# Batch 3's loads gated on the second half of batch 2's q^T in an attention kernel with a feed-forward stage

## The chip, the cores and the metric

One core of a Trainium2 chip. The metric is device time in microseconds (us) of one execution. Times are medians over several executions of the same kernel, with the lowest and highest where that matters.

## The reference

```python
# q, k, v: (batch 8, heads 8, seq 1024, head_dim 64); E, F: (64, 1024)
k_proj = einsum('ks,bhsd->bhkd', E, k)          # 1024 keys become 64
v_proj = einsum('ks,bhsd->bhkd', F, v)
attn   = softmax(q @ k_proj^T / 8)
x      = (attn @ v_proj).transpose(0, 2, 1, 3).reshape(8192, 512)
out    = maximum(x @ w1, x @ w2) @ w_out        # (8192, 512), float32
```

## The kernel before

TensorE carries the whole kernel: projections, scores, values and the feed-forward products of one batch are interleaved by hand in a fixed order of "slots". The attention of batch b runs among the feed-forward products of the batch before it. What the argument needs is who moves the data of the next batch.

**GpSimd issues the loads**, 1 MB each, in the order k, v, q. Four buffers rotate among all k, v and q tiles, so a load must wait until the last reader of the buffer that it takes over is done.

```python
kvq = ctx.enter_context(tc.tile_pool(name="kvq", bufs=4))
...
def step_gate(t, n, *at):        # a 1x1 copy: GpSimd stands here until that part of the tile is written
    nc.gpsimd.tensor_copy(out=junk, in_=t[n][(slice(0, 1), *at, slice(0, 1))])
```

**SyncE issues the transposes by DMA and all stores**, in one queue, in order. q^T comes in two halves (heads 0 to 3 and heads 4 to 7); from batch 3 on the projected keys are transposed by DMA too (kpt).

```python
def step_qt_dma(t, h0=0, h1=H):
    nc.sync.dma_start_transpose(out=t["qt"][:, h0:h1]..., in_=t["q"][:, h0:h1]...)   # cut
def step_kpt_dma(t):
    nc.sync.dma_start_transpose(out=t["kpt"], in_=t["kp"]...)                        # cut
```

**The schedule.** `("P", 0, p, i)` is a slot of the down products of the first unit (half a batch), `("U", n, h, i)` one of the up products under unit n, `("G", n, h)` the place of a group of scores. The line marked "the gate: head 3" is the one that the change touches. (Comments are added, and the lines that set up a batch's tiles are cut.)

```python
t = tiles[2]
at_slot(("P", 0, 1, 0), step_qt_dma, t, 0, H // 2)              # first half of q^T
at_slot(("U", 1, 0, 1), step_kv, t, 0, H, "kv", True)
at_slot(("U", 1, 0, 4), step_kpt, t, 0, H, True)                # batch 2: kpt by TensorE
at_slot(("G", 1, 0), step_qt_dma, t, H // 2, H)                 # second half, behind the stores
at_slot(("U", 1, 0, 6), step_gate, t, "qt", H // 2 - 1)         # the gate: head 3
at_slot(("U", 1, 0, 6), loads, 3, "k", "v", "q")

for b in range(3, B):
    t = tiles[b]; n = 2 * b - 3
    key = ("G", n, 0) if b == 3 else ("U", n - 1, 1, 5)
    at_slot(key, step_qt_dma, t, 0, H // 2)
    at_slot(key, step_qt_dma, t, H // 2, H)
    at_slot(("U", n, 0, 1), step_kv, t, 0, H, "kv", True, True) # its end issues kpt by DMA
    at_slot(("U", n, 0, 6), step_gate, t, "qt", H - 1)          # the gate: head 7
    at_slot(("U", n, 0, 6), step_gate, t, "kp", H - 1, 1)
    at_slot(("U", n, 0, 6), loads, b + 1, "k", "v", "q")
```

From batch 3 on, both halves of q^T, then a store, then kpt go through SyncE's queue, and the first scores of the batch need kpt.

The softmax here doesn't subtract the row's maximum and nothing guards it: scores larger than these inputs give would overflow.

Of the kernel before, what the change touches and what calls it, by code (L numbers as in the profile page):

```python
# [16 lines left out]
def kernel(  # L17
# [14 lines left out]
    B, H, S, D = q.shape  # L32
# [436 lines left out]
    U = {(b, o): {"n": n, "b": b, "o": o, "t": tiles[b]} for n, (b, o) in enumerate(units)}  # L469
# [263 lines left out]
    t = tiles[0]  # L733
# [100 lines left out]
    def at_slot(key, s, *a):  # L834
        steps.setdefault(key, []).append(lambda: s(*a))
# [11 lines left out]
    t = tiles[1]  # L847
# [26 lines left out]
    t = tiles[2]  # L874
# [2 lines left out]
    at_slot(("U", 1, 0, 1), step_kv, t, 0, H, "kv", True)  # L877
    at_slot(("U", 1, 0, 4), step_kpt, t, 0, H, True)
    at_slot(("G", 1, 0), step_qt_dma, t, H // 2, H)
    at_slot(("U", 1, 0, 6), step_gate, t, "qt", H // 2 - 1)  # L880
    at_slot(("U", 1, 0, 6), loads, 3, "k", "v", "q")

    for b in range(3, B):
        t = tiles[b]
# [77 lines left out]
```

## Time and profile before

| | before |
|---|---|
| median of 3 runs | 325.81 us (325.14 to 325.97) |
| span of the profiled run, its clock | 323.2 us, 1.000 |
| TensorE busy | 316.0 us, 98% |

The prediction shows most of the lines of this kernel's profile. Here are those that it left out. First, from the page, the granted TensorE clock in 40 slices (9 is 90% or more of full speed), and the chain that ended last by engine:

```profile
PEclk9999999999999999999999999999999999999999
...
PE 84%; DMA 9%; DVE 2%; POOL 2%; issue 1%; SPq 1%; ACT 0%; DVEq 0%; POOLq 0%
```

The clock is full throughout and the chain is TensorE's own work for 84% of the span. The waits of TensorE after 60 us (line, releaser, then us in total, times, longest):

```profile
PE mm_ps L275 <- DMA qt_sb<-q_sb: 0.3, 1, 0.3
```

In 260 us TensorE waits once, for 0.3 us. The DMA queues from 77.9 to 81.7 us (packets, MB, share of the 16 engines):

```profile
DMA packets 562, 0.56 MB, mean 148 GB/s; under 512 B 28, under 2 KB 561, under 8 KB 561
...
q0 software_dynamic: 465, 0.48, 91.8%
```

q0 is GpSimd's queue of loads.

### The profile page before, as it was taken

To read this page: it belongs to the slowest core of one execution; us is meant where nothing else is said; L and a number is where in the kernel's file an instruction comes from. 1 tells how busy PE (TensorE), PEld (TensorE's weight loads), DVE (VectorE), ACT (ScalarE), POOL (GpSimd) and SP (SyncE) were. 2 spreads that over 40 slices of the span, in tenths; PEclk is the share of its full clock that TensorE was granted. 3 is DMA by queue.
4 is the path that set the end of the run, shared out by engine and by line. 5 is a ranking of instruction groups with operands and counts; after the bars stand their busy time and mean duration, and the time that the engine had idled before them with its cause. 6 is when DMAs were issued, how large, how long until landed. Compare 5 with 4: busy or idle time off the path is not lost.

```text
span 323.2 us, 9033 instructions
## 1 busy us (share of the span) xinstructions
PE 316.0 (98%) x3852; PEld 248.4 (77%) x3852; DVE 236.8 (73%) x420; ACT 203.1 (63%) x364; POOL 41.6 (13%) x65
## 2 busy tenths in 40 slices
PE   8989999999999999999999999999999999999995
PEld 3554457878887888878887888878887888888884
DVE  1365798896867797877967796977967796969572
ACT  1466532667676777667776777657776777764541
POOL 8649002001200300030000300030000000000000
PEclk9999999999999999999999999999999999999999
DMA  8999999999999799699979999689969130312133
GB/s 160 207 196 185 204 204 204 207 203 179 256 216 213 135 203 244 143 177 144 234 147 201 154 211 231 115 180 183 232 130 213 38 100 32 99 34 98 34 121 108
DMA packets 76280, 53.14 MB, mean 164 GB/s; under 512 B 29520, under 2 KB 76112, under 8 KB 76240
## 3 DMA queue, kind: packets, MB, share of 16 engines
q0 software_dynamic: 30976, 28.31, 56.0%
q1 hardware_dynamic: 45264, 24.25, 31.2%
q8 instruction: 30, 0.49, 0.6%
q14 instruction: 10, 0.08, 0.1%
HBM read 57.15 MB, written 16.78 MB: 229 GB/s over the span
## 4 chain that ended last, share of the span: by engine, by line
PE 84%; DMA 9%; DVE 2%; POOL 2%; issue 1%; SPq 1%; ACT 0%; DVEq 0%; POOLq 0%
PE mm_ps L649 43%; PE mm_ps L571 24%; PE att_ps L188 4%; DMA v_sb<-in_v_dram 4%; DMA qt_sb<-q_sb 3%; PE mm_ps L415 3%; PE att_ps L287 3%; PE mm_ps L275 3%; PE mm_ps L453 2%; DMA big<-in_moe_w_dram 2%; POOL q_sb L102 1%; POOL k_sb L102 1%; DVE gt_sb L586 1%; PE mm_ps L246 1%; PE mm_ps L440 1%
## 5 line engine op out<-in xcount | busy, mean ns | idle before, releaser
L542 ACT COPY p_sb<-mm_ps 128x512 f32<-128x512 f32 x172 | 97.2, 594 | 42.0 <-PE mm_ps L571 30.0
L649 PEld LDWEIGHTS <-big 128*128 128x128 f16 x768 | 73.5, 98 | 12.0 <-issue 3.5
L649 PE MATMUL mm_ps<-T_sb,big 128*128 128x256 f16 x576 | 77.9, 273 | 0.0
L586 DVE TENSOR_TENSOR gt_sb<-mm_ps,p_sb 128x512 f16<-128x512 f32 x56 | 38.6, 688 | 45.5 <-PE mm_ps L571 42.7
L571 PE MATMUL mm_ps<-big,big 128*128 128x256 f16 x336 | 50.4, 273 | 0.0
L571 PEld LDWEIGHTS <-big 128*128 128x128 f16 x448 | 43.8, 98 | 5.2
L649 PEld LDWEIGHTS <-gt_sb 128*128 128x128 f16 x384 | 35.8, 98 | 9.9 <-issue 5.4
L649 PE MATMUL mm_ps<-wo_sb,gt_sb 128*128 128x256 f16 x256 | 43.0, 273 | 0.1
L571 PEld LDWEIGHTS <-wd_sb 128*128 128x128 f16 x336 | 32.9, 98 | 3.8
L571 PE MATMUL mm_ps<-xt_sb,wd_sb 128*128 128x256 f16 x224 | 33.6, 273 | 0.0
L364 ACT ACTIVATE ex_sb<-mm_ps 128x512 f16<-128x512 f32 x50 | 27.2, 597 | 10.2 <-PE att_ps L287 8.1
L390 DVE TENSOR_TENSOR xt_sb<-att_ps,ld_sb 128x1024 f16<-128x1024 f32 x26 | 31.7, 1219 | 0.1
L673 DVE TENSOR_TENSOR o_sb<-mm_ps,p_sb 128x512 f32<-128x512 f32 x32 | 21.9, 685 | 7.7 <-PE mm_ps L649 7.7
L649 PE MATMUL mm_ps<-m_sb,xt_sb 128*128 128x256 f16 x128 | 24.4, 273 | 0.0
L238 POOL COPY junk<-qt_sb 1x1 f16<-1x1 f16 x6 | 1.7, 284 | 169.6 <-DMA qt_sb<-q_sb 169.6
L621 ACT ACTIVATE gt_sb<-mm_ps 128x512 f16<-128x512 f32 x28 | 16.8, 600 | 8.7 <-PE mm_ps L571 8.7
L532 DVE TENSOR_TENSOR big<-gt_sb 128x1024 f16<-128x1024 f16 x32 | 21.9, 685 | 0.3
L589 DVE TENSOR_SCALAR gt_sb<-gt_sb 128x512 f16<-128x512 f16 (+1 forms) x56 | 20.4, 365 | 1.9
L649 PE MATMUL mm_ps<-wo_sb,big 128*128 128x256 f16 x128 | 21.5, 273 | 0.0
L649 PE MATMUL mm_ps<-T_sb,gt_sb 128*128 128x256 f16 x128 | 21.5, 273 | 0.0
L649 PEld LDWEIGHTS <-xt_sb 128*128 128x128 f16 x192 | 18.8, 98 | 2.2
L586 DVE TENSOR_TENSOR gt_sb<-p_sb 128x512 f16<-128x512 f32 x28 | 19.1, 682 | 0.0
(88 smaller groups left out, 429.5 us busy)
## 6 DMA issues: line engine op xcount, KB each, us to landing
out_dram<-o_sb SPq DMA_DIRECT2D x63, 256.0 KB, 2.7
k_sb<-in_k_dram POOLq DMA_DIRECT2D x7, 1024.0 KB, 11.3
v_sb<-in_v_dram POOLq DMA_DIRECT2D x7, 1024.0 KB, 16.7
q_sb<-in_q_dram POOLq DMA_DIRECT2D x5, 1024.0 KB, 22.8
q_sb<-in_q_dram POOLq DMA_DIRECT2D x4, 512.0 KB, 19.4
big<-in_moe_w_dram POOLq DMA_DIRECT2D x12, 128.0 KB, 8.6
k_sb<-in_k_dram POOLq DMA_DIRECT2D x4, 256.0 KB, 6.1
q_sb<-in_q_dram POOLq DMA_DIRECT2D x4, 256.0 KB, 7.2
```

What stands on the lines that cost most here:

```text
L188: nc.tensor.matmul(out=kv_ps[r * KP : (r + 1) * KP, 0:n], lhsT=eft[:, i, c, :], rhs=t[w][:, h0:h1, c, :], start=(c == 0), stop=(c == NC - 1),)
L275: nc.tensor.matmul(out=banks[e][pos : pos + Z, h * W : (h + 1) * W], lhsT=t["kpt"][o * D : (o + 1) * D, head, s * Z : (s + 1) * Z], rhs=t[ ...
L364: nc.scalar.activation(out=t["ex", g, j][:, e, :], in_=banks[e], func=ACTF.Exp, scale=scale)
L390: nc.vector.tensor_tensor(out=x_out(t, g, j).rearrange("q z o n -> q o z n"), in0=at_ps.rearrange("q o (z n) -> q o z n", z=2), in1=ld[:, ...
L532: nc.vector.tensor_tensor(out=S(i), in0=x, in1=y, op=op)
L542: copy(out=x, in_=bank)
L571: nc.tensor.matmul(out=bank[:, m * W : (m + 1) * W], lhsT=w_[:, n_, (2 * d + m) * 128 : (2 * d + m + 1) * 128], rhs=a[:, n_, :], start=(n ...
L586: nc.vector.tensor_tensor(out=c_blk(j, c), in0=two(x), in1=two(y), op=ALU.add)
L589: nc.vector.tensor_scalar_max(ap, ap, 0.0)
L621: nc.scalar.activation(out=out, in_=in_, func=ACTF.Relu)
L649: nc.tensor.matmul(out=bank[:, i * CH : (i + 1) * CH], lhsT=a(c)[:, i * 128 : (i + 1) * 128], rhs=w_(c), start=(n is not None and m == (lo ...
L673: nc.vector.tensor_tensor(out=o_sb, in0=two(x), in1=two(y), op=ALU.add)
```

## The change

Before, GpSimd may load batch 3 once the first half of batch 2's q^T is there. Then k3's packets come onto the shared DMA engines before the second half has landed, and its landing is late (10.66 us after issue). The intent is to keep k3 out of its way; v3 has to wait for the second half in any case.

```diff
     at_slot(("G", 1, 0), step_qt_dma, t, H // 2, H)
-    at_slot(("U", 1, 0, 6), step_gate, t, "qt", H // 2 - 1)
+    at_slot(("U", 1, 0, 6), step_gate, t, "qt", H - 1)
     at_slot(("U", 1, 0, 6), loads, 3, "k", "v", "q")
```

## The prediction

> **What bounds the kernel now.** I read the page first (busy shares, the chain that ended last), then the waits, then the GpSimd, SyncE and DMA views of the 65 to 115 us stretch, which is where the changed line acts.
>
> ```profile
> span 323.2 us, 9033 instructions
> PE 316.0 (98%) x3852; PEld 248.4 (77%) x3852; DVE 236.8 (73%) x420; ACT 203.1 (63%) x364; POOL 41.6 (13%) x65
> ```
>
> TensorE is busy 98% of the span, in program order. So a transfer costs time only if a matmul has to wait for it, and a wait that is taken away gains only what TensorE lost there. The chain that ended last is matmuls with one DMA piece in this stretch, and TensorE's timeline shows what that piece is worth:
>
> ```profile
> 72.17 10.66 DMA qt_sb<-q_sb
> ...
> 82.88 0.41 PE L275 MATMUL mm_ps<-qt_sb,kpt_sb 64*32 64x256 f16 x16 [0.31 <-DMA qt_sb<-q_sb]
> ...
> 110.21 0.62 PE L275 MATMUL mm_ps<-qt_sb,kpt_sb 64*32 64x256 f16 x16
> ```
>
> The second half of batch 2's q^T is issued at 72.17 and lands 10.66 us later, at 82.83. The scores of heads 4 to 7 of batch 2 wait 0.31 us for it: that is all TensorE loses there. The last line is the first score group of batch 3, which needs batch 3's kpt; it starts without a wait. GpSimd, which issues the loads:
>
> ```profile
> 71.82 0.61 POOL L238 COPY junk<-qt_sb 1x1 f16<-1x1 f16 x1 [19.08 <-DMA qt_sb<-q_sb]
> 73.04 0.90 POOL L102 DMA_DIRECT2D k_sb<-in_k_dram  x1 [0.62 <-PE mm_ps L571]
> 83.40 0.87 POOL L102 DMA_DIRECT2D v_sb<-in_v_dram  x1 [9.46 <-DMA qt_sb<-q_sb]
> 84.27 0.88 POOL L102 DMA_DIRECT2D q_sb<-in_q_dram  x1
> ```
>
> The gate (the 1x1 copy) opens when the first half has landed. k3 (batch 3's k) follows at once. But v3 waits another 9.46 us for the second half: it takes over the buffer of batch 2's q, which the second transpose still reads. Only k3 profits from the early gate. SyncE, which issues transposes and stores in order:
>
> ```profile
> 75.71 23.78 SPq L664 DMA_DIRECT2D out_dram<-o_sb  x8
> 100.17 5.70 SPq L258 DMA_TRANSPOSE qt_sb<-q_sb  x2
> 105.96 0.53 SPq L664 DMA_DIRECT2D out_dram<-o_sb  x1
> 106.97 1.20 SPq L232 DMA_TRANSPOSE kpt_sb<-kp_sb  x1
> ```
>
> The DMA view gives issue to landing: k3 14.8 us (73.04 to 87.84), v3 11.6 (to 95.05), q3 15.8 (84.27 to 100.12), kpt3 2.7 (106.97 to 109.68). So batch 3's transposes start at 100.17 **because q3 lands at 100.12**; kpt3 follows on the same queue and lands 0.53 us ahead of the matmul at 110.21. This chain, loads to q3 to transposes to kpt3 to scores, is hidden now with half a microsecond to spare.
>
> One more view decides how much of k3's early issue is real. The DMA queues from 73.1 to 77.2 us, and then from 77.2 to 79 us:
>
> ```profile
> q1 hardware_dynamic: 2262, 0.85, 101.9%
> ```
>
> ```profile
> q0 software_dynamic: 119, 0.12, 76.8%
> q1 hardware_dynamic: 177, 0.05, 12.6%
> ```
>
> In the first window only the hardware queue (stores and transposes) moves anything, with all engines taken. k3's first packet runs at 77.26, 4.2 us after its issue, just as the packets of the second half run out (74.26 to 77.86). So the data of that half is there at 77.9; its completion comes only at 82.83. Behind the first half the completion came about 0.5 us after its last packet (71.25, landed 71.76). The 5 us are new: in them k3's packets and four stores have come onto the same engines.
>
> **What the Trainium skill says.** "DMA: Bandwidth & Descriptors", section "Issuing engines are not separate DMA queues": DMAs from GpSimd and SyncE run on the same 16 engines and interleave. The trace agrees (k3's 4.2 us, the 10.66 us landing). The same page, "Queues, rings and completion order": the increment of the semaphore lands only after the earlier writes of that engine, across its queues. That fits a completion that is late once k3's writes run; the trace shows the lateness, not its cause. "TensorE: Matmul & The Clock Gate", section "What's actually happening": after an idle window of about 3.4 us the clock falls to half, until some 3.4 us of work. This trace cannot show it: the granted clock is 1.000 and TensorE has no such gap here.
>
> **The change part by part.** It adds and removes no instruction: the gate reads head 7 of q^T instead of head 3, so it waits for the second transpose.
>
> 1. The second half is issued at 72.17 as before (it waits for SyncE's order and q2, which landed at 69.86). Its packets end at 77.8 as before; with no loads behind it its completion follows in about 0.6 us: it lands at **78.4** instead of 82.83. (6.2 us; the other halves take 4.3 to 6.4 where they are not in loads.) TensorE's wait at 82.88 goes: **-0.31 us**.
> 2. Gate to first load: in the later batches, where the gate already reads head 7, k goes out 0.85, 0.99, 1.34 and 1.14 us after the landing (108.81 for 107.96, 143.40 for 142.41, 179.56 for 178.22, 215.09 for 213.95); mean 1.1. k3 is issued at **79.5** instead of 73.04, v3 at 80.4 and q3 at 81.2, both earlier than now.
> 3. Three loads in a row: from the issue of k to the landing of q it takes 24.0, 24.8, 24.6 and 24.6 us in those batches (108.81 to 132.79 and so on), each with four stores beside it. Take 24.5: q3 lands at **104.0** instead of 100.12. A check from the packets: k3's first packet would run 1.7 us after issue (110.52 for 108.81), at 81.2 instead of 77.26, so the whole stream moves by 3.9 us; it now runs 77.26 to 99.77 without a break. v3 would land near 98, before step_kv at 102.7.
> 4. Batch 3's transposes are issued at 104.05. From q3's landing to kpt3's landing it is 9.56 us now (100.12 to 109.68): two transposes, a store, kpt3, all in order on one queue. So kpt3 lands at about **113.6**. Without the change TensorE would want it at 110.21, with the gain of step 1 at 109.9. It starts at about 113.6, a wait of 3.7 us.
> 5. Net: 113.6 less 110.21, rounded to **+3.4 us**. After it TensorE has no slack to make it up: it waits for nothing until the tail.
> 6. Batch 4: its gate opens with the q^T of batch 3, near 111.8 instead of 107.96, so q4 lands near 136.8 (now 132.79). Its transposes were issued at 134.42 and move with TensorE to 137.8. Still in time; the loss is paid once.
>
> 325.81 + 3.4 = **329.2 us**.
>
> **The rivals.** (a) *A small gain*: the gate only takes k3 out of the way of the second half, everything else is hidden, 325.5 us. For it speaks that v3 and q3 go out three microseconds earlier than now, and that DMA looks busy, not late. Against it: the three loads share the same engines, so what counts is when the stream starts, and q3 is the last of it; the slack at the end is 0.5 us. It would need q3 to land by about 100.6. (b) *The stream is shorter than I take it*: the store of 75.71 finishes before the loads, and the transposes no longer disturb the ramp. Then q3 lands near 102.5 and the loss is 1.9 us, 327.7. (c) *The clock drops*: the wait of 3.7 us is just longer than the window that the skill names, which runs freely, so usually no full window is idle; if one is, some 1.7 us more, 331. (d) *Batch 4 late too*: step 6 leaves 1 us; if it fails, up to 1 us more.
>
> **Range and chances.** The largest uncertainty is step 3, about 1 us either way, then step 4, some 0.5 us, then (c) and (d) upward. Eight times in ten 326.9 to 331.4. Two per cent is 6.5 us: slower than 332.3 needs (c) and (d) together, 4%; faster by 2% is out of reach, since what is taken away is 0.31 us, 1%.
>
> **What would show it.** Step 1: the second half lands near 78.4, and the wait before the matmul near 82.9 is gone. Step 2: all three loads in a row from about 79.5, without a wait between. Step 3: q3 lands near 104. Step 4: SyncE's pair of transposes moves to about 104 and TensorE waits 3 to 4 us for kpt3 (or its transposed batch 3) near 110, the one new gap. Step 6: no gap at batch 4. I am wrong if the second half still lands near 83 (then k3 starts near 84 and the loss is about 8 us), or if q3 lands before 101 (no loss).

## The result and the profile after

| | before | after |
|---|---|---|
| median (lowest to highest), 6 runs each in the same rounds | 325.81 us (325.12 to 327.21) | 330.00 us (327.72 to 331.42) |
| ratio, 95% interval | | 1.0124 (1.0084 to 1.0165) |
| span and clock of the profiled run | 323.2 us, 1.000 | 329.7 us, 0.990 |

A ratio here is the mean time of one kernel's runs over the mean of the other's in the same rounds, so it is not quite the ratio of the medians. The profiled run of the kernel after is the slowest of its six (331.42); the median run is 1.4 us shorter. So sizes are read from two profiles, this one and one of the same kernel run again.

The page of the kernel after:

```profile
span 329.7 us, 9033 instructions
PE 319.1 (97%) x3852; PEld 249.8 (76%) x3852; DVE 236.4 (72%) x420; ACT 203.4 (62%) x364; POOL 41.2 (12%) x65
...
PEclk9999999999999879999999999999999999999999
```

The instructions are as many as before. TensorE's busy time grew by 3.1 us with the same work, and the clock row says where most of it came from: two slices, from 107 to 124 us, are no longer at full speed.

GpSimd's timeline of the stretch (start, us, engine, line, operation; in brackets the idle time before and its releaser):

```profile
79.49 0.18 POOL L238 COPY junk<-qt_sb 1x1 f16<-1x1 f16 x1 [26.14 <-DMA qt_sb<-q_sb]
80.72 0.90 POOL L102 DMA_DIRECT2D k_sb<-in_k_dram  x1 [1.05 <-PE mm_ps L571]
81.60 0.89 POOL L102 DMA_DIRECT2D v_sb<-in_v_dram  x1
82.46 0.90 POOL L102 DMA_DIRECT2D q_sb<-in_q_dram  x1
```

The gate opens at 79.49 where it opened at 71.82, and the loads go out in a row: k3 7.7 us later than before, v3 and q3 1.8 us earlier. Now the DMA queues in the same 3.8 us as above, 77.9 to 81.7:

```profile
DMA packets 20, 0.02 MB, mean 4 GB/s; under 512 B 4, under 2 KB 20, under 8 KB 20
```

This is where the time comes from. **The 16 DMA engines stand nearly idle** (4 GB/s for 148) between the second half's data and k3's. Until 79.44 the half's completion is awaited; then the gate, the issue (80.72) and the start of the load take their time. Stores move again from 82.06, and k3's first packet runs at 82.94, 5.7 us later than in the kernel before (77.26). The loads that follow are the same 3120 packets of q0, first in the 77.2 to 100.15 us of the kernel before, then in the 82.9 to 105.9 us of the kernel after:

```profile
q0 software_dynamic: 3120, 3.15, 86.5%
```

```profile
q0 software_dynamic: 3120, 3.15, 86.6%
```

The stream starts 5.7 us later and is as long as before: from its first packet to the landing of q3 it takes 22.9 us in both kernels. Hence q3 lands at 105.86 instead of 100.12. SyncE's queue after:

```profile
75.92 24.31 SPq L664 DMA_DIRECT2D out_dram<-o_sb  x8
105.91 4.57 SPq L258 DMA_TRANSPOSE qt_sb<-q_sb  x2
110.57 0.75 SPq L664 DMA_DIRECT2D out_dram<-o_sb  x1
111.42 1.22 SPq L232 DMA_TRANSPOSE kpt_sb<-kp_sb  x1
```

The pair of transposes moved from 100.17 to 105.91, and kpt3 (batch 3's kpt) from 106.97 to 111.42. TensorE's timeline:

```profile
83.30 0.41 PE L275 MATMUL mm_ps<-qt_sb,kpt_sb 64*32 64x256 f16 x16
...
114.27 0.63 PE L275 MATMUL mm_ps<-qt_sb,kpt_sb 64*32 64x256 f16 x16 [3.46 <-DMA kpt_sb<-kp_sb]
114.83 2.74 PE L649 MATMUL mm_ps<-T_sb,big 128*128 128x256 f16 x12
```

The first line is the score group that waited 0.31 us before: no wait now (it stands at 83.30 because this run was 0.8 us behind by 49 us already). The second is batch 3's first: 3.46 us of wait, new. The third is a bill that follows: twelve products take 2.74 us. In the kernel before the same twelve took half:

```profile
110.76 1.48 PE L649 MATMUL mm_ps<-T_sb,big 128*128 128x256 f16 x12
```

The trace's clock record is at 0.5 from 112.87 us for 6.83 us. The list of TensorE's waits after 60 us has a single entry, as before, but ten times the size:

```profile
PE mm_ps L275 <- DMA kpt_sb<-kp_sb: 3.5, 1, 3.5
```

Laying TensorE's 3852 matmuls of both kernels side by side, one for one, the shift of the kernel after changes in three places after the start: -0.38 us at the matmul of 82.88, +3.64 at that of 110.21, then +2.4 while the clock is at half. (The other 0.8 us of the 6.4 at the end arose before 49 us, ahead of anything that the change touches.)

### The profile page after: what moved, and what is told of

The parts are those of the page before. It is cut to its first block, busy times and chain, and to the rows that moved or that the text cites.

```text
span 329.7 us, 9033 instructions
## 1 busy us (share of the span) xinstructions
PE 319.1 (97%) x3852; PEld 249.8 (76%) x3852; DVE 236.4 (72%) x420; ACT 203.4 (62%) x364; POOL 41.2 (12%) x65
## 4 chain that ended last, share of the span: by engine, by line
PE 89%; DMA 4%; DVE 3%; POOL 2%; issue 1%; DVEq 0%; POOLq 0%
PE mm_ps L649 45%; PE mm_ps L571 26%; PE mm_ps L415 4%; PE att_ps L188 4%; DMA v_sb<-in_v_dram 4%; PE att_ps L287 3%; PE mm_ps L275 3%; PE mm_ps L453 2%; DVE gt_sb L586 1%; POOL q_sb L102 1%; DMA kpt_sb<-kp_sb 1%; POOL k_sb L102 1%; PE mm_ps L246 1%; PE mm_ps L440 1%; DVE xt_sb L338 0%
## 5 line engine op out<-in xcount | busy, mean ns | idle before, releaser
L649 PE MATMUL mm_ps<-T_sb,big 128*128 128x256 f16 x576 | 79.2, 276 | 0.0
L571 PE MATMUL mm_ps<-xt_sb,wd_sb 128*128 128x256 f16 x224 | 34.4, 277 | 0.0
```

Source lines behind the costliest of these rows:

```text
L571: nc.tensor.matmul(out=bank[:, m * W : (m + 1) * W], lhsT=w_[:, n_, (2 * d + m) * 128 : (2 * d + m + 1) * 128], rhs=a[:, n_, :], start=(n ...
L649: nc.tensor.matmul(out=bank[:, i * CH : (i + 1) * CH], lhsT=a(c)[:, i * 128 : (i + 1) * 128], rhs=w_(c), start=(n is not None and m == (lo ...
```

## The experiments

All kernels gave correct results in the fast state. Each was timed beside the kernel before on the same chip (medians of before: 325.19, 325.68 and 325.37 us in the three batches of runs). Unless said otherwise the edit is made in the kernel after.

| run | median us | ratio to before (95%) | q3 lands | TensorE's wait at batch 3's first scores |
|---|---|---|---|---|
| the change, again | 330.38 | 1.0138 (1.0088 to 1.0189) | 105.68 | 4.11 |
| kpt of batch 3 by TensorE | 326.82 | 1.0041 (1.0012 to 1.0070) | 105.35 | none |
| the wait filled with useless matmuls | 328.90 | 1.0109 (1.0081 to 1.0137) | 105.54 | 0.33 |
| second half right behind the first | 325.53 | 1.0017 (0.9979 to 1.0055) | 100.76 | none |
| second half behind one store | 325.02 | 0.9980 (0.9947 to 1.0013) | 100.18 | none |
| the same, again | 325.11 | 0.9994 (0.9973 to 1.0015) | 100.11 | none |
| second half behind three stores | 326.14 | 1.0014 (0.9988 to 1.0040) | 101.37 | 0.63; 0.90 at 219 |
| kpt of batch 3 between the halves | 328.76 | 1.0106 (1.0062 to 1.0150) | 106.50 | 1.98 |
| before, without the gate | 329.22 | 1.0104 (1.0076 to 1.0133) | 102.26 | none; 2.93 at 77.6 |
| before, second half behind one store | 324.85 | 0.9985 (0.9956 to 1.0013) | 101.44 | none |
| one store, later gate on kpt | 326.07 | 1.0019 (0.9990 to 1.0047) | 100.72 | none; 0.92 at 219 |

### The change again

> The changed kernel once more, for its spread. Theory: TensorE waits 2 to 4 us for batch 3's kpt near 110 us, and a run is longer still when this wait halves the clock for one or two windows. Then runs with a mean clock of 1.000 lie near 328, with 0.995 near 330, with 0.990 near 331.4. Rival: the spread of the changed kernel (327.7 to 331.4) has nothing to do with the clock; then time and clock are not ordered alike.

The kernel unchanged (a blank line added): 330.62, 330.94, 330.14 and 327.45 us. TensorE's line:

```profile
114.44 0.56 PE L275 MATMUL mm_ps<-qt_sb,kpt_sb 64*32 64x256 f16 x16 [4.11 <-DMA kpt_sb<-kp_sb]
```

The shift is -0.38 us at 82.88 and +4.29 at 110.21; then the clock is at half for 3.41 us (+1.4). So the mechanism repeats. The mean clocks of the ten runs sort their times: 327.45 and 327.72 at 1.000, 329.76 to 330.62 at 0.995, 330.94 and 331.42 at 0.990. In the two profiles half the clock for 3.41 us is a mean of 0.995, and for 6.83 us 0.990. So eight of ten runs probably paid for one or two stretches at half clock behind the wait. Only the two profiles show where the stretch lies; for the other six it is inferred from the mean, and 6 of the 29 runs of the kernel before that were timed beside the experiments had a mean of 0.995 too.

### The wait itself: batch 3's kpt by TensorE

```diff
-        at_slot(("U", n, 0, 1), step_kv, t, 0, H, "kv", True, True)
+        at_slot(("U", n, 0, 1), step_kv, t, 0, H, "kv", True, b > 3)
+        if b == 3:
+            at_slot(("U", n, 0, 4), step_kpt, t, 0, H, True)
...
-        at_slot(("U", n, 0, 6), step_gate, t, "kp", H - 1, 1)
+        if b > 3:
+            at_slot(("U", n, 0, 6), step_gate, t, "kp", H - 1, 1)
```

> The changed kernel, but batch 3's kpt is made by TensorE and VectorE as batch 2's is, instead of the transposing DMA that stands behind both halves of q^T on SyncE's queue. Loads and gate stay as late as in the changed kernel (q3 lands near 105.5). Theory (the late loads cost time only through kpt3's place in that queue): the wait near 110 us shrinks to under 0.6 us (for the first half of q^T, which lands near 110.3), 16 more matmuls cost 0.4 us, clock 1.000, 325.7 to 326.7 us. Rival (late loads cost through k3 and v3, or by slowing all transfers): still 328.5 us or more.

The loads stay as late as in the kernel after (q3 at 105.35), only kpt3 no longer queues behind q^T. TensorE's timeline at batch 3, and at batch 4:

```profile
110.46 0.40 PE L275 MATMUL mm_ps<-qt_sb,kpt_sb 64*32 64x256 f16 x16
...
147.54 0.41 PE L275 MATMUL mm_ps<-qt_sb,kpt_sb 64*32 64x256 f16 x16 [1.27 <-DMA kpt_sb<-kp_sb]
```

The wait near 110 is gone, and with it most of the loss: 326.82 us where the change took 330.38, at the price of 16 transposes (+0.46 us). So at batch 3 late loads cost TensorE nothing by themselves; they cost through kpt3. (The edit also drops the second gate of batch 3, the one on kp.) The wait at 147.54, and another one of 0.99 us at batch 6, is something else: in this run kpt4 and kpt6 landed 4.5 and 4.4 us after issue instead of 2.7. The last experiment returns to it.

### The clock: the wait filled

```diff
             banks = [mm_bank(n=2 + e) for e in range(2)]
+            if t is tiles[3] and (g, j) == (0, 0):
+                for _ in range(14):
+                    nc.tensor.matmul(
+                        out=banks[0], lhsT=ones16[:, 0:128], rhs=ones16, start=True, stop=True
+                    )
             score(t, g, j, banks)
```

> The changed kernel with 14 matmuls of 512 columns that nobody needs just before the first scores of batch 3, that is, inside the wait: some 3.0 us of work. Theory (part of the loss is the clock, which falls because TensorE idles for 3.5 us): clock 1.000 in every run, the wait that is left under 1 us, 328.3 to 329.5 us, so 0.5 to 1.5 us faster than the changed kernel although it does more. Rival 1 (the clock falls for another reason): 330 us as the changed kernel and the clock still 0.995. Rival 2 (the wait is not where I say): the matmuls add their 3 us, 333 us.

TensorE now works through the wait, for nothing:

```profile
110.40 3.20 PE L353 MATMUL mm_ps<-ones 128*128 128x512 f16 x14
113.92 0.41 PE L275 MATMUL mm_ps<-qt_sb,kpt_sb 64*32 64x256 f16 x16 [0.33 <-DMA kpt_sb<-kp_sb]
114.27 1.49 PE L654 MATMUL mm_ps<-T_sb,big 128*128 128x256 f16 x12
```

The scores still start at 113.92, since kpt3 is no earlier, but the twelve products behind them take 1.49 us again, not 2.74. Two rows of the busy table by stretch for 105 to 120 us show the same (the clock is the third number from the end), the kernel after and then this one:

```profile
105.00:120.00 15.00, 11.54 (x116) 8.58 (x115) 6.10 (x10) 7.28 (x13) 2.98 (x5) 0.77 0.88 156
```

```profile
105.00:120.00 15.00, 14.67 (x153) 11.07 (x152) 8.90 (x15) 8.25 (x16) 2.98 (x5) 1.00 0.86 152
```

The idle time caused the half clock: doing more work there removes it. All four runs had a mean clock of 0.998 or 1.000, where eight of ten runs of the kernel after had 0.995 or less. In time the run is 328.90 us for 330.38. The intervals of the two ratios overlap, so the clocks carry this point rather than the medians. (This profile also had a late kpt6, a wait of 1.0 us near 222.)

### The order on SyncE's queue: the second half earlier

Four stores stand between the two halves of q^T in SyncE's queue. If the late gate costs time only because the second half is late, an earlier second half must give the loss back with the gate left as in the kernel after.

```diff
     at_slot(("P", 0, 1, 0), step_qt_dma, t, 0, H // 2)
+    at_slot(("P", 0, 1, 0), step_qt_dma, t, H // 2, H)
-    at_slot(("G", 1, 0), step_qt_dma, t, H // 2, H)
```

> The changed kernel, but the second half of batch 2's q^T is issued directly behind the first, ahead of four stores on SyncE's queue. The gate still waits for the second half. Theory (what counts is when the stream of three loads starts): the second half lands near 75 instead of 79.4, k3 is issued near 76.2 and q3 lands near 101, the wait for kpt3 is 0 to 0.8 us, 325.5 to 326.5 us. Rival (waiting for the second half is itself the cost, for example because k3 no longer overlaps it): 328.5 us or more. A third: four stores that now go 3 us later stop VectorE or ScalarE for want of output buffers; then a new wait on those buffers shows, with 1 to 3 us.

The second half lands at 74.60, k3 is issued at 75.89, q3 lands at 100.76, and TensorE waits for nothing after 60 us: 325.53 us, no different from before. So the second half's time, not the gate's choice of half, carries the loss.

A smaller dose, `("P", 0, 4, 1)` in place of `("G", 1, 0)`, puts the half behind one of the four stores:

> A dose between the changed kernel and half2_first: the second half of batch 2's q^T goes behind one of the four stores instead of behind all four (changed kernel) or none (half2_first). Theory (one for one: the later the gate opens, the later q3 lands, the longer the wait for kpt3): the second half lands near 76.5 (79.2 in the changed kernel, 74.6 in half2_first), q3 lands near 102.7 (105.7, 100.8), TensorE waits 1 to 2 us for kpt3 (3.5 to 4.1, 0), the clock stays at 1.000 because that is shorter than in the changed kernel, 326 to 327.3 us. Rival (a threshold, not a line): either no wait or the whole 3.5 us.

The wait that I expected did not come. The half landed at 75.21 (76.5 expected), and the whole stream was shorter than I had allowed for: q3 at 100.18, not 102.7. The dose was too small to tell anything about the slope, but GpSimd's timeline shows something better:

```profile
75.26 0.18 POOL L238 COPY junk<-qt_sb 1x1 f16<-1x1 f16 x1 [22.36 <-DMA qt_sb<-q_sb]
76.49 0.90 POOL L102 DMA_DIRECT2D k_sb<-in_k_dram  x1 [1.05 <-PE mm_ps L649]
77.38 0.88 POOL L102 DMA_DIRECT2D v_sb<-in_v_dram  x1
78.24 0.90 POOL L102 DMA_DIRECT2D q_sb<-in_q_dram  x1
```

k3 is issued here 3.45 us later than in the kernel before (73.04) and lands 1.4 us earlier (86.40 for 87.84); q3 lands at the same time. The early issue of k3 in the kernel before was worth next to nothing: its first packet ran at 77.26 there and at 78.12 here, and from it to q3's landing it took 22.9 and 22.1 us.

Because 325.02 us looked a little better than before, it was run again with more runs:

> half2_up once more with more rounds, as a candidate against the kernel before: gate on the second half, the second half behind one store. Theory: TensorE loses nothing at 82.9 and nothing at 110, so it is 0.2 to 0.6 us faster than the kernel before, 0.1 to 0.2 per cent. Rival: the difference seen in half2_up (0.2 per cent, not clear of noise) was chance; then the ratio lies at or over 1.000.

325.11 us, ratio 0.9994: if there is a gain it is not clear of the noise. At `("P", 0, 5, 1)` the half was meant to go behind three stores, for a middle dose:

> The dose that half2_up missed: the changed kernel with the second half of batch 2's q^T behind three of the four stores. In half2_up (behind one) it landed at 75.2 and q3 at 100.2, without a wait; in the changed kernel (behind four) at 79.2 and q3 at 105.8, with a wait of 3.5 to 4.1 us. Theory (one for one beyond a slack of about half a microsecond, so no wait while q3 lands before 100.7): the second half lands near 77.3, q3 near 102.7, the wait for kpt3 is 1 to 2.5 us, the clock stays full in most runs, 326 to 327.5 us. Rival (a threshold): no wait at all or all 3.5 us.

```profile
110.68 0.41 PE L275 MATMUL mm_ps<-qt_sb,kpt_sb 64*32 64x256 f16 x16 [0.63 <-DMA kpt_sb<-kp_sb]
```

The half landed at 75.59, again earlier than meant, and q3 at 101.37, which gives a wait of 0.63 us. With the others this makes a row for kernels whose TensorE comes to this place at nearly the same time (110.0 to 110.8): q3 at 100.1 to 100.2, no wait; 101.37, 0.63 us; 105.7 to 105.9, 3.5 to 4.1 us. The slack ends near 100.7, and from there the wait grows with q3, not quite one for one.

### The other order: kpt3 before the second half of batch 3

```diff
-        at_slot(key, step_qt_dma, t, H // 2, H)
+        at_slot(("U", n, 0, 3) if b == 3 else key, step_qt_dma, t, H // 2, H)
```

> The changed kernel, but batch 3's kpt goes to SyncE's queue between the two halves of its q^T instead of behind both. Nothing else moves; q3 lands near 105.7. Theory: kpt3 lands near 112 instead of 114.3, TensorE waits 1 to 2 us instead of 3.5 to 4.1, the clock mostly stays full, 326.3 to 328 us. Rival (kpt3 is bound by its own data, not by its place behind the second half): as the changed kernel, 329.5 us or more.

```profile
112.45 0.41 PE L275 MATMUL mm_ps<-qt_sb,kpt_sb 64*32 64x256 f16 x16 [1.98 <-DMA kpt_sb<-kp_sb]
```

```profile
149.91 0.41 PE L275 MATMUL mm_ps<-qt_sb,kpt_sb 64*32 64x256 f16 x16 [1.54 <-DMA kpt_sb<-kp_sb]
```

These two groups are the first scores of batch 3 and of batch 4. The first wait shrinks from 3.5 to 4.1 us to 1.98, which confirms that a transpose ahead of kpt3 in the queue costs 1.5 to 2.1 us there. But now the second half of batch 3 lands at 115.27, the gate of batch 4 opens late, k4 goes out at 116.12 (113.51 in the kernel after), and batch 4 has a wait of its own. The loss moved on instead of going away: 328.76 us.

### The gate of before, taken away and helped

Removing the gate line from the kernel before lets k3 go as soon as its buffer is free:

```diff
-    at_slot(("U", 1, 0, 6), step_gate, t, "qt", H // 2 - 1)
```

> The kernel before without any gate for batch 3's loads: k3 is issued as soon as its buffer is free, near 60 us, so its data comes right behind q2's, while the first half of q^T is being transposed; v3 and q3 still wait for the second half through v3's buffer. Theory (a load that comes onto the engines beside a transpose makes the completion of that transpose late, as k3 did to the second half in the kernel before): the first half lands 3 us or more later than 71.8, the first scores of batch 2 (near 74.5) wait for it, 1 to 4 us slower than before, 326.5 to 330 us. Rival (the gate is not needed, the transpose only queues for its share): the first half lands before 74, no wait there, 324.5 to 326 us.

GpSimd's and TensorE's timelines:

```profile
58.71 0.90 POOL L102 DMA_DIRECT2D k_sb<-in_k_dram  x1 [5.97 <-PE mm_ps L649]
83.96 0.88 POOL L102 DMA_DIRECT2D v_sb<-in_v_dram  x1 [24.35 <-DMA qt_sb<-q_sb]
```

```profile
77.62 0.63 PE L275 MATMUL mm_ps<-qt_sb,kpt_sb 64*32 64x256 f16 x16 [2.93 <-DMA qt_sb<-q_sb]
78.18 1.89 PE L649 MATMUL mm_ps<-T_sb,big 128*128 128x256 f16 x8
```

k3 goes out at 58.71, and now the first half of q^T pays: it takes 10.87 us from issue to landing (5.1 in the kernel before) and TensorE waits 2.93 us for it. The clock falls here too (half for 3.41 us from 77.5; eight products take 1.89 us). 329.22 us: a load that is too early costs as much as one that is too late. The gate of before was set between the two.

What k3 does to the second half in the kernel before can be read from the packets. The half's data end at 77.86. From 77.9 to 79.7 us only loads move:

```profile
DMA packets 148, 0.15 MB, mean 84 GB/s; under 512 B 0, under 2 KB 148, under 8 KB 148
...
q0 software_dynamic: 148, 0.15, 80.0%
```

The next packets of SyncE's queue are of 4 bytes, from 79.79 on; the first store packet follows at 80.44. So k3's packets stood between the half's data and its landing at 82.83.

In the kernel before with its own gate, the second half moved behind one store:

```diff
-    at_slot(("G", 1, 0), step_qt_dma, t, H // 2, H)
+    at_slot(("P", 0, 4, 1), step_qt_dma, t, H // 2, H)
     at_slot(("U", 1, 0, 6), step_gate, t, "qt", H // 2 - 1)
```

> The kernel before (gate on the first half), with the second half of batch 2's q^T behind one store instead of four. Theory: the second half's data is through before k3's packets arrive or soon after, so it lands before 82.5 and the 0.3 us wait at 82.9 goes; q3 lands at or before 100, no wait for kpt3; 0.1 to 0.5 us faster than before, inside the noise of one run. Rival (the stores that go later cost as much): same time or slower.

The 0.31 us wait is gone (shift -0.38 us at 82.88) and 324.85 us is the lowest median, but its interval (0.9956 to 1.0013) reaches past 1. With the half moved up, early and late gate (0.9985; 0.9980 and 0.9994) can't be told apart.

### Late landings of kpt: a race with the next loads?

In some profiles kpt of batch 4 or 6 landed 4.2 to 4.5 us after issue instead of 2.7. My theory was that the next batch's loads overtake it, as k3 does with the second half. So the gate behind kp was moved to the finished kpt, in the kernel with the half behind one store:

```diff
-        at_slot(("U", n, 0, 6), step_gate, t, "kp", H - 1, 1)
+        at_slot(("U", n, 0, 6), step_gate, t, "kpt", H - 1)
```

> half2_up, and from batch 3 on the second gate reads the finished kpt instead of kp, so the next loads are issued about 2 us later, when kpt has landed. In three of the profiles kpt of a later batch landed 4.4 or 3.1 us after its issue instead of 2.7, and TensorE waited 1.2 to 1.8 us. Theory (the next loads come onto the engines while kpt is under way, a race): with this gate kpt lands 2.7 us after its issue in every batch; the next q lands 2 us later, which just uses up the 1.6 to 2.2 us that it has, so 324.8 to 326.2 us with less spread. Rival (the later loads cost more than the race): q lands too late in every batch and TensorE waits for kpt in each, 327 us or more.

TensorE's wait after 60 us in this run, and the DMA queues between kpt6's issue (214.75) and its landing (218.97):

```profile
PE mm_ps L275 <- DMA kpt_sb<-kp_sb: 0.9, 1, 0.9
```

```profile
q1 hardware_dynamic: 753, 0.33, 33.8%
q8 instruction: 1, 0.02, 1.6%
...
kpt_sb<-kp_sb SPq DMA_TRANSPOSE x1, 4.2
```

**The theory fell.** No load runs in that window (there is no q0 row), and kpt6 still took 4.2 us. What does run there is one packet of 16 KB of the instruction queue, q8, for 1.1 us on one engine (1.6% of 16 engines for 4.2 us). In the 13 profiles kpt is transposed by DMA 64 times after 60 us. A q8 packet ran during each of the five late landings, and began during two of the 59 others, in their last 0.5 us. The second half of q^T took 6.95 to 7.31 us in the kernel after, in its repeat and in the three variants that leave that half in its place, and there too a q8 packet ran at the end of the transpose. That is a coincidence in every case, not an experiment: no run here moved the fetch alone.

The order of the packets goes a step further. In this run the q8 packet runs from 216.83 to 217.94, and from 217.01 to 217.91 no packet starts. The last packets before kpt6 lands are these, from 217.91 to 218.97:

```profile
DMA packets 2, 0.00 MB, mean 0 GB/s; under 512 B 2, under 2 KB 2, under 8 KB 2
```

They are two of 4 bytes, at 217.92 and 217.93, just as the q8 packet ends. In the run with the half behind one store, the q8 packet near kpt6 began at 216.96, when the last 4-byte packet ran as well, and kpt6 was quick (2.75 us). So it is likely that the fetch held up the end of the transpose. Why the landing then came 1.04 us after the last packet, and 0.44 us in the quick case, stays open.

## Why the prediction was right, and where not

The predicted time, 329.2 us, is 0.8 us under the median of 330.0, and the range held all but the very edge: the slowest run, 331.42, is 0.02 us above it. That it came so close is in part luck: the two runs at full clock lie 1.5 and 1.8 us under 329.2, the eight with a lowered clock 0.6 to 2.2 us over it.

1. **The second half without loads behind it.** Predicted 78.4, measured 79.44 (78.91 again). The wait at 82.88 went as said (-0.38 us in both for -0.31). The microsecond too much coincides with the instruction packet named above: it ran from 77.37 to 78.25, and two packets of 4 bytes at 78.23 and 78.24, the first of SyncE's queue after 77.90. That it is the cause is not shown. That the loads made the landing late in the kernel before is seen in the order of its packets, and supported by the kernel without a gate, where an earlier k3 did the same to the first half.
2. **Gate to issue.** Predicted 1.1 us, measured 1.28. The three loads went out in a row, as said.
3. **q3.** Predicted 104.0, measured 105.86. Of the 1.86 us, 1.04 came from step 1, 0.18 from step 2, and 0.64 from the time between the issue of k3 and the landing of q3, 25.14 us and not 24.5. Most of this lies before the first packet: it ran 2.22 us after the issue, at 82.94, where the prediction's check took 1.7 us and 81.2. The stream itself was no longer than before.
4. **kpt3.** Predicted 113.6, measured 114.22. This was closer than q3 because an error went the other way: the path from q3 to kpt3 took 8.36 us, and I had kept the 9.56 of before. The wait of 3.7 us was 3.46 and 4.11.
5. **The net.** The step, that the shift at batch 3 is +3.4, was about right: -0.38 + 3.64 = 3.3 and -0.38 + 4.29 = 3.9. But the sum ended there, and **the clock was the term that was mis-sized**. Rival (c) called a full idle window unusual; eight of ten runs had a mean clock of 0.995 or less, and both profiles show the half clock behind the wait (+2.4 and +1.4 us). The reason I gave was wrong as well: I took the window of about 3.4 us, which the skill names, as one that must be wholly idle. In the kernel without a gate TensorE idled from 74.69 to 77.62, shorter than that window, and the clock was down at 77.5. The net without the clock is seen in the two runs at clock 1.000: 327.72 and 327.45, which is 1.9 and 2.3 us over before, and so less than the two profiles' 3.3 and 3.9. What the wait was in those runs no profile shows.
6. **Batch 4 in time.** Right for the change itself: q4 landed at 137.42, kpt4 at 151.99, no wait. Rival (d), that the lateness is handed on to batch 4, appeared when kpt3 was put between the halves.

Rival (a), everything else hidden, fell: q3 came 5.7 us later. Rival (b), a shorter stream of loads, fell for this change (22.9 us from the first packet to q3's landing in both kernels).

The prediction said that the trace before cannot show what the skill says of the clock; these runs can. "TensorE: Matmul & The Clock Gate", section "What's actually happening", gives about 3.4 us as the window by which the clock is set. The stretches at half clock lasted 3.41 us (twice) and 6.83 us, so the length of the window agrees. The prediction also took k3's 4.2 us as agreeing with the interleaving that the skill states. They show that the engines are shared; but from 73.1 to 77.2 us only SyncE's queue moved, which is not interleaving.

## What to carry to other kernels

An early load isn't worth having for its issue time: look when its first packet moves and when the last of its group lands, and follow that through the queue of whoever waits for it, here kpt behind two transposes and a store. A gate that waits for a completion leaves the DMA engines nearly idle until new packets come (4 GB/s from 77.9 to 81.7 us here, and the first load packet at 82.94), so where there is no slack move the awaited transfer forward in its queue rather than the gate back. And a wait of about 3 to 4 us on TensorE is to be reckoned with a second item, the clock at half for 3.4 or 6.8 us, which here added 1.4 to 2.4 us in most runs (a wait of 1.98 us did not bring it).

## What the Trainium skill lacked or had wrong

- "TensorE: Matmul & The Clock Gate" names at least one idle window of about 3.4 us as what lowers the clock, and in its advice gaps over about 3 us. Here 2.93 us of idle time were enough (clock at half 2.81 us after TensorE stopped), and in the profile of the change the clock fell 2.06 us into the wait. Gaps of 1.98 and 1.54 us did not lower it. So a partly idle window can do; what share is needed no run here shows.
- "DMA: Bandwidth & Descriptors" says that transfers of different engines interleave, but no page gives the time that loads on the same engines add to a transpose's landing: 10.66 us for the second half of q^T with k3 behind it and 7.0 without, 10.87 for the first half with k3 ahead of it and 5.1 without.
- No page says how long a load issued beside a busy transpose queue stands still: k3 moved no packet for 4.2 us after its issue in the kernel before, and for 1.6 to 2.3 us in the kernels whose gate waits for the second half.
- "Runtime: NRT & Kernel Launch", section "Instruction fetch mechanics", says that instructions are fetched over a DMA queue in blocks of 16 KiB, at a cost mostly hidden. The 16 KB packets of the instruction queue here, of about 1 us, agree; what they do to transfers beside them no page says. In the five late landings of kpt (4.2 to 4.5 us for 2.7) one ran during the transpose. That it is the cause is likely by the order of the packets, and shown by no experiment.
